# Loading order and early tiles at the opening of a one-core attention and gated-MLP kernel

## The chip, the cores and the metric

One core of a Trainium2 chip runs the whole program in one launch. The metric is the device time of one execution in microseconds. Three runs of the kernel before gave 556.28, 556.47 and 556.8, median 556.47. The engines are called PE (matrix products), PEld (PE's weight loads), DVE, ACT, POOL and SP; SP issues most transfers.

## The reference, cut to what matters

The input x has 2048 rows of 576. It is normalized per row, and two branches take the result: windowed causal attention (32 heads of 18, window 256) with an output product, and an MLP whose gate is a sigmoid. The output is x + attention * silu(MLP).

```python
def _A_ref(x, wqkv, wo):
    H = 32; Dh = D // H; W = 256
    q, k, v = qkv[0], qkv[1], qkv[2]
    scores = jnp.einsum("bhqd,bhkd->bhqk", q, k) * (Dh ** -0.5)
    mask = (idx[:, None] - idx[None, :] >= 0) & (idx[:, None] - idx[None, :] < W)
    p = _softmax(jnp.where(mask[None, None], scores, -1e9), axis=-1)
    return (lambda x, *d: x.transpose(*d))(o, 0, 2, 1, 3).reshape(B, S, D) @ wo

def _B_ref(x, w_gate, w_up, w_down):          # D = 576, F = 4608
    h = _sigmoid(g) * u                       # g = x @ w_gate, u = x @ w_up
    return jnp.einsum("bsf,fd->bsd", h, w_down)

xn = _layernorm(x, axis=-1)
s = _A_ref(xn, A_wqkv, A_wo)
g = _silu(_B_ref(xn, B_w_gate, B_w_up, B_w_down))
return x + s * g
```

## The kernel before

The rows are taken in four stretches (`c`, 512 rows each, four blocks of 128). In each stretch x is normalized and transposed to `xnT`; then come the v and q/k products, 40 tiles of scores with their exponentials on ACT and masks on DVE, two runs of PV products (L817), the output product of attention, 36 tiles of gate and up ("F tiles", 128 hidden units each), and the down products with the final combination.

**Products in pairs.** The contraction of 576 is split into four blocks of 128 and a remainder of 64. Every matmul uses 64 rows of the array, and `pair` (L123) issues two of them that run side by side. A gate/up tile is two turns: `lo` (four pairs, the 128-row blocks) and `hi` (the same four for the other halves, and the pair of the remainder, `wgr`). The second turn waits for the first, so PE does another turn in between where one is at hand.

**The planner.** `build_graph` lists operations with dependencies, estimates and priorities. `schedule` (L1125) then places them one by one on the engines, each on the engine's earliest start plus 10 ns for each step of priority, and so fixes the order of every engine; `emit` writes the program in that order, with waits on semaphores. On the chip an engine never overtakes: an operation that is late holds all behind it on its engine. The planner's estimates have no other effect than on this order.

**PSUM.** There are four units of two banks each. `pool_s` (units 0 and 1) serves transposes, q/k, v, scores and the attention output; `pool_f` (2, 3 and 1) serves F tiles and down products; `pool_v` all four, for PV. A unit is taken by the operation that comes first and given back by the copy that empties it (L361 to L363). The planner bars a pool from a unit that a more urgent claim of the other wants.

**The opening** (stretch 0). SP issues by priority: the four x blocks (`load_x`, `X_PRIO`, L70), then the weights of tiles 0 and 1 (gate, up, and the remainders with `REM_PRIO`), then the next groups of two tiles (`weights`, L923). Each x block is normalized on its own (`build_ln`, L525): statistics on DVE, block 2's on ACT (`STATS_ACT`), a power on POOL, the normalization and a 64-column duplicate on DVE, ten small transposes on PE (L613), and a copy from PSUM to `xnT` on the engine that `XE_ENG` names (L590). The statistics of the fourth block have a low priority (`LN_PRIO`, 16). Until the first transposes PE runs products on zeros (`NWARM` pairs, L490). Then the first `NEARLY` F tiles are made in parts, so that PE can start on the blocks that are there: `PARTS` (L80) gives the ranges of blocks. Each early tile holds its own PSUM unit until its last part, and the `lo` turn of the following tile, `ahead` (L995), is put in front of the last part's `hi`.

**Instruction loads.** PE's program is read in pieces of 256 instructions. A PV run is very dense in instructions, and `fits` (L1113) lets it start only where the next piece has, by the planner's reckoning, the time `FETCH_NS` to arrive. `SPACE_NS` is the least distance between score tiles that the planner aims at, `FILL_NS` how much it pays for it, `POOL_IN_NS` the margin for a unit's release.

Of the kernel before, what the change touches and what calls it, by code (L numbers as in the profile page):

```python
# [8 lines left out]
D = 576  # L9
# [37 lines left out]
RUN_NS = 6.3  # L47
STEP_NS = (54.0, 30.6)
# [21 lines left out]
X_PRIO = (0, 0, 0, 0)  # L70
# [4 lines left out]
XE_ENG = ("ACT", "ACT", "ACT", "DVE")  # L75
NWARM = (43, 10)
NEARLY = 2
FIRST_SLACK_NS = (-800.0, -1500.0)
BUSY_SLACK_NS = 1500.0
PARTS = (((0, 1), (1, 2), (2, 3), (3, 4)),) * NEARLY  # L80
# [10 lines left out]
POOL_IN_NS = 140.0  # L91
DMA_PE_NS = 690.0
FILL_NS = 100.0
SPACE_NS = (1700, 1800, 1700, 1700)
# [101 lines left out]
class Op:  # L196
    __slots__ = ("eng", "est", "deps", "fn", "name", "prio", "start", "end", "tok", "needs_tok",
                 "nbytes", "slack", "idx", "succs", "cidx", "odeps", "acq", "lane", "filler", "space", "ni", "run", "then")

    def __init__(self, eng, est, fn, name, deps, prio, nbytes, odeps, acq):  # L200
        self.eng = eng
        self.est = float(est)
        self.fn = fn
        self.name = name
        self.deps = []
        seen = set()
        stack = list(deps)
        while stack:
            d = stack.pop(0)
            if d is None:  # L210
                continue
            if isinstance(d, (list, tuple)):
                stack = list(d) + stack
            elif id(d) not in seen:
                seen.add(id(d))
                self.deps.append(d)
        self.prio = prio
        self.start = None
        self.end = None
        self.tok = None  # L220
        self.needs_tok = False
        self.nbytes = nbytes
        self.idx = -1
        self.succs = []
        self.cidx = -1
        self.odeps = [d for d in odeps if d is not None]
        self.acq = acq
        self.lane = None
        self.slack = 0.0
        self.filler = None  # L230
        self.space = 0.0
        self.ni = 0
        self.run = 0
        self.then = None
        for d in self.odeps:
            assert d.eng == eng
# [22 lines left out]
class Builder:  # L259
# [40 lines left out]
    def alloc_memory(self):  # L300
# [61 lines left out]
        self.pool_f = Pool("F", [2, 3, 1], last)  # L362
# [55 lines left out]
    def load_x(self, c, i=0):  # L418
        if c == 0:
            for i in range(BPC):  # L420
                self.x_dma[i] = (self.dma(self.x0[:, i, :], self.x[i * P:(i + 1) * P, :], P * D * 2, f"dma:x{i}", ("x0", i), prio=X_PRIO[i]),
                                 self.x0[:, i, :])
                self.x_dma[i][0].slack = -220.0
# [20 lines left out]
    def load_rem(self, dst, srcs, name, lane, prio, deps=()):  # L444
        return [self.dma(dst[ROWS[1 - t], :], src[0:RD, :], RD * src.shape[1] * 3, name, lane + (t,), deps=deps, prio=prio)
# [150 lines left out]
    def act_stats(self, x_in, o_x, pr):  # L596
# [4 lines left out]
        m = op("POOL", 150, lambda e: e.tensor_scalar(nm, sx, -1.0 / D, None, ALU.mult), "ln:am", deps=[a1], prio=pr)  # L601
        a2 = op("ACT", act_ns(D) + 150, lambda e: e.activation(junk, x_in, ACTF.Square, bias=nm, accum_out=sq), "ln:aq", deps=[m], prio=pr)
        v = op("POOL", 150, lambda e: e.tensor_scalar(ve, sq, 1.0 / D, EPS, ALU.mult, ALU.add), "ln:av", deps=[a2], prio=pr)
# [301 lines left out]
    def build_ffn(self, c):  # L905
# [17 lines left out]
        def weights(wg):  # L923
# [14 lines left out]
            if c == 0:  # L938
                for d in ds:
                    d.slack = FIRST_SLACK_NS[0] if wg == 0 else BUSY_SLACK_NS if wg > 6 else 0.0  # L940
                for d in rem:
                    d.slack = FIRST_SLACK_NS[1] if wg < 2 else BUSY_SLACK_NS if wg > 6 else 0.0

# [10 lines left out]
        def gate_up(ft, h, half, acq, part=None, deps=(), behind=()):  # L954
# [8 lines left out]
            def f(eng):  # L963
                return turn(eng, [bank(h, w)[:, t0:t0 + n] for w in range(2)], lhs, lambda r, t, k: x_in[r, k, t0:t0 + n], half)
            o = op("PE", len(BLOCKS[half]) * mm_ns(n), f, f"f1{half}:{c}:{ft}", deps=[xin, wops[ft // WG][0:1 + half], deps],
                   prio=3 if part is None else 1, odeps=chain[half] if part is None else list(behind), acq=acq,
# [19 lines left out]
        if early:  # L986
# [3 lines left out]
            for ft, h in enumerate(hs):  # L990
                u = None
                for part in range(len(PARTS[ft])):
                    lo = gate_up(ft, h, 0, None if part else h, part, [u])
                    if ft == early - 1 and part == len(PARTS[ft]) - 1:
                        ahead = self.pool_f.hold()  # L995
# [117 lines left out]
    def fits(self, at, n, st, places, ffn):  # L1113
# [5 lines left out]
        while edge - FETCH - FETCH_AHEAD < at + n:  # L1119
            if edge > at and when(edge) - when(edge - FETCH - FETCH_AHEAD) < FETCH_NS[ffn]:  # L1120
# [4 lines left out]
    def schedule(self):  # L1125
# [13 lines left out]
        last_sc = 0.0  # L1139
        at = 2  # L1140
# [5 lines left out]
        while nsched < len(ops):  # L1146
            best = None
            for e in ENGS:
# [10 lines left out]
                for o in cand:  # L1159
# [3 lines left out]
                    if o.run and not self.fits(at + len(self.new_waits(o, known)) // 2, o.run, st, places, int(ffn[phase] < FETCH)):  # L1163
# [52 lines left out]
            if o.lane is not None:  # L1216
# [3 lines left out]
                bw_clock = max(bw_clock, stt + o.est) + o.nbytes / DMA_BYTES_PER_NS  # L1220
            else:
# [120 lines left out]
```

## Time and profile before

| what | us |
|---|---|
| profiled execution, device time | 556.48 |
| its span | 555.2 |
| PE busy | 549.9 (99%) |
| DVE busy | 325.1 (59%) |
| ACT busy | 271.7 (49%) |
| POOL busy | 208.8 (38%) |
| first product on real data starts | 7.98 |
| first product of 512 columns starts | 12.23 |
| last product ends | 552.7 |

How to read it: times within the execution count from the span's start. Busy shares are averages over the whole span. The chain that ended last is followed back from the last instruction, at each step to what released it. In a row of the timeline stand the start, the length, engine and line, the operation, what it writes and reads, how many instructions are merged in the row, and in brackets the idle time before it with what ended it. Idle time of an engine that is not the bottleneck costs nothing.

### The profile page before, as it was taken

How to read it: one execution, taken by the hardware profiler on the slowest of the kernel's cores; microseconds unless marked ns; L12 is line 12 of the kernel's file. 1: busy time of each engine (PE TensorE's matmuls, PEld its weight loads, DVE VectorE, ACT ScalarE, POOL GpSimd, SP SyncE). 2: the span in 40 equal slices, each digit the busy share in tenths (PEclk: the TensorE clock that was granted, in tenths of full speed). 3: DMA queues.
4: the chain of work that ended last, by engine and by line, in shares of the span. 5: the costliest groups of instructions: out<-in, count | busy, mean ns of one | idle time of the engine just before them, and what ended most of it. 6: DMA issues, size and time to landing. Idle time of an engine off the chain costs nothing.

```text
span 555.2 us, 19412 instructions
## 1 busy us (share of the span) xinstructions
PE 549.9 (99%) x8342; PEld 341.2 (61%) x8342; DVE 325.1 (59%) x782; ACT 271.7 (49%) x379; POOL 208.8 (38%) x360
## 2 busy tenths in 40 slices
PE   8999999999999999999999999999999999999998
PEld 7454455777555655577855565447877655445887
DVE  5467677745966545746565557664455657653511
ACT  4246554432566543645265563764165555765021
POOL 5634353826271230554452322745063332700300
DMA  8899999542256664462126653663013464540001
GB/s 230 234 263 239 248 241 257 150 91 59 72 164 182 198 167 132 129 161 53 32 65 193 201 162 101 185 179 87 9 34 103 119 204 138 153 134 2 20 28 46
DMA packets 141213, 75.87 MB, mean 137 GB/s; under 512 B 43676, under 2 KB 139260, under 8 KB 141128
## 3 DMA queue, kind: packets, MB, share of 16 engines
q1 hardware_dynamic: 133704, 68.71, 47.3%
q0 software_dynamic: 7424, 5.92, 4.0%
q8 instruction: 66, 1.08, 0.8%
q14 instruction: 19, 0.16, 0.1%
HBM read 63.18 MB, written 2.36 MB: 118 GB/s over the span
## 4 chain that ended last, share of the span: by engine, by line
PE 98%; DMA 1%; SPq 0%; issue 0%; DVE 0%; ACT 0%
PE ps L127 95%; PE ps L817 3%; DMA wgs<-in_B_w_up_dram 1%; SPq L290 0%; ACT thf L1087 0%; PE ps L613 0%; DVE thf L1089 0%; DVE xf L1092 0%
## 5 line engine op out<-in xcount | busy, mean ns | idle before, releaser
L127 PE MATMUL ps<-xnT,wgs 64*128 64x512 bf16 (+1 forms) x2400 | 284.0, 368 | 0.6 <-DMA wgs<-in_B_w_up_dram 0.5
L767 ACT ACTIVATE expr<-ps 128x1024 bf16<-128x1024 f32 (+4 forms) x160 | 155.0, 968 | 81.0 <-PE ps L127 80.5
L127 PEld LDWEIGHTS ps<-xnT,wgs 64*128 64x128 bf16 x2400 | 114.7, 94 | 108.6 <-issue 1.1
L127 PE MATMUL ps<-wd_sb,hT 64*128 64x288 bf16 (+2 forms) x2448 | 152.7, 276 | 0.0
L290 POOL DMA_DIRECT2D qk<-qd x160 | 82.9, 524 | 161.7 <-PE ps L127 152.9
L977 DVE SCALAR_TENSOR_TENSOR hT<-tring,ps 128x512 bf16<-128x512 bf16 x144 | 98.6, 685 | 74.2 <-ACT tring L974 72.6
L974 ACT ACTIVATE tring<-ps 128x512 bf16<-128x512 f32 x144 | 86.2, 598 | 113.9 <-PE ps L127 112.3
L127 PEld LDWEIGHTS ps<-wd_sb,hT 64*128 64x128 bf16 x2448 | 113.0, 94 | 29.4
L780 DVE TENSOR_TENSOR expr<-expr,mask 128x128 bf16<-128x128 bf16 (+2 forms) x240 | 65.2, 299 | 62.0 <-ACT expr L767 59.4
L290 POOL DMA_DIRECT2D oT<-o2T x72 | 36.8, 520 | 115.3 <-DVE ot L848 52.4
L731 POOL TENSOR_SCALAR kx<-kprev,small 128x256 bf16<-128x256 bf16 x64 | 60.1, 949 | 6.0 <-PE ps L127 5.1
L127 PE MATMUL ps<-qk,kx 64*128 64x320 bf16 (+1 forms) x704 | 59.2, 254 | 0.0
L127 PE MATMUL ps<-xnT,wgr 64*128 64x512 bf16 (+1 forms) x300 | 56.0, 367 | 0.0
L127 PEld LDWEIGHTS ps<-qk,kx 64*128 64x128 bf16 x704 | 31.9, 94 | 26.6
L127 PE MATMUL ps<-xnT,wqg 64*128 64x512 bf16 (+1 forms) x320 | 37.7, 355 | 0.0
L652 DVE CAST qd<-ps 128x1024 bf16<-128x1024 f32 (+1 forms) x20 | 22.3, 1115 | 11.1 <-PE ps L127 11.1
L845 DVE STREAM_TRANSPOSE ot<-ps 128x512 f32<-128x512 f32 x32 | 20.3, 687 | 13.9 <-PE ps L817 13.8
L127 PEld LDWEIGHTS ps<-xnT,wgr 64*128 64x128 bf16 x300 | 15.0, 94 | 16.4
L731 DVE TENSOR_SCALAR kx<-qk,small 128x512 bf16<-128x512 bf16 x64 | 21.9, 370 | 5.4 <-PE ps L127 4.9
L853 DVE STREAM_TRANSPOSE o2T<-o 128x512 bf16<-128x512 bf16 x32 | 22.6, 706 | 3.0 <-DMA oT<-o2T 2.5
L127 PEld LDWEIGHTS ps<-xnT,wqg 64*128 64x128 bf16 x320 | 15.0, 94 | 11.5 <-issue 0.4
L1080 ACT ACTIVATE thf<-ps 128x576 bf16<-128x576 f32 x12 | 7.8, 650 | 27.4 <-PE ps L127 27.4
(68 smaller groups left out, 289.3 us busy)
## 6 DMA issues: line engine op xcount, KB each, us to landing
wgs<-in_B_w_gate_dram SPq DMA_DIRECT2D x72, 256.0 KB, 3.5
wgs<-in_B_w_up_dram SPq DMA_DIRECT2D x72, 256.0 KB, 4.0
wd_sb<-in_B_w_down_dram SPq DMA_DIRECT2D x9, 576.0 KB, 6.7
wqg<-in_A_wqkv_dram SPq DMA_DIRECT2D x32, 128.0 KB, 3.8
qk<-qd POOLq DMA_DIRECT2D x100, 36.0 KB, 2.7
wgr<-in_B_w_gate_dram SPq DMA_DIRECT2D x36, 64.0 KB, 3.1
wgr<-in_B_w_up_dram SPq DMA_DIRECT2D x36, 64.0 KB, 2.9
wvo<-in_A_wqkv_dram SPq DMA_DIRECT2D x4, 576.0 KB, 4.2
```

What stands on the lines that cost most here:

```text
L127: res = eng.matmul(outs[i], lhs(ROWS[t], i), rhs(ROWS[t], i), start=start, stop=stop, tile_position=(64 * t, 0))
L290: o = self.op(eng, DMA_ISSUE_NS[eng], lambda e: e.dma_start(dst, src), name, deps, prio, nbytes=nbytes)
L652: return eng.tensor_copy(dst, self.both(h, n))
L731: return e.tensor_scalar(self.kx[:, sx, pos:pos + n_ // SW, t, :], src.rearrange("p (s k) -> p s k", k=SW), self.half[:, t:t + 1], None, A ...
L767: return eng.activation(self.expr[:, se, :, lo * SW:NT], self.both(h, NT)[:, :, lo * SW:NT], ACTF.Exp, scale=SM_SCALE)
L780: return eng.tensor_tensor(e_, e_, m_, ALU.mult)
L817: res = eng.matmul(outs[i][p0:p0 + VH, cols], self.v_aug[ROWS[i], o:o + VH], self.expr[ROWS[i], se, t, cols], start=m == 0, stop=m == len( ...
L845: return e.transpose(self.ot1[:, p1, :], self.halves(hp, NT, un)[i])
L853: t2 = op("DVE", dve_ns(NT), lambda e, p2=p2, p3=p3: e.transpose(self.o2T[:, p3, :], self.o2[:, p2, :]), f"ot2:{c}:{pr}:{i}", deps=[on, d3 ...
L974: th = op("ACT", act_ns(NT), lambda e: e.activation(self.tring[:, st, :], bank(h, 0), ACTF.Tanh, scale=0.5), f"th:{c}:{ft}", deps=[pg, dt_ ...
L977: mu = op("DVE", dve_ns(NT), lambda e: e.scalar_tensor_tensor(self.hT[:, ft, :], self.tring[:, st, :], 1.0, bank(h, 1), ALU.add, ALU.mult) ...
L1080: th = op("ACT", act_ns(w), lambda e: e.activation(v2(t), y2(), ACTF.Tanh, scale=0.25), f"fth:{nm}", deps=[f2, dt_], prio=0)
```

## The change

Five things are edited.

1. The fourth x block's load gets the priority 1.8, which puts it behind the first gate, up and remainder weights and in front of the second weight group.
2. `NEARLY` goes from 2 to 3; the third early tile has two parts, blocks 0 to 2 together and block 3. Parts of early tiles get a priority that grows with the tile.
3. The first block's copy from PSUM moves from ACT to DVE (`XE_ENG`).
4. `pool_f` takes unit 0 as well, as its last choice; the tile run ahead in the opening is confined to unit 0 (`pool_a`).
5. The planner's numbers: the landing of the opening's transfers is now estimated by a running sum of bytes and a latency for each (`OPEN_NS`, `X_LAT_NS`, `W_LAT_NS`), score tiles are spaced by 1900 to 2000 ns, a unit's margin is 120 ns, two estimates on POOL are larger, there is one more warm-up pair, and the rule for PV runs relaxes with the time that a run has waited (`RELAX_NS`).

```diff
RUN_NS = 6.3
+RELAX_NS = 200e3
 STEP_NS = (54.0, 30.6)
...
 LN_PRIO = (0, 0, 0, 16)
-X_PRIO = (0, 0, 0, 0)
+X_PRIO = (0, 0, 0, 1.8)
 REM_PRIO = 0.6
...
 DUP_ACT = ()
-XE_ENG = ("ACT", "ACT", "ACT", "DVE")
-NWARM = (43, 10)
-NEARLY = 2
-FIRST_SLACK_NS = (-800.0, -1500.0)
+XE_ENG = ("DVE", "ACT", "ACT", "DVE")
+NWARM = (44, 10)
+NEARLY = 3
+OPEN_NS = 2000.0
+OPEN_BYTES_PER_NS = 256.0
+X_LAT_NS = (400.0, 600.0, 900.0, 800.0)
+W_LAT_NS = (650.0, 1100.0)
 BUSY_SLACK_NS = 1500.0
-PARTS = (((0, 1), (1, 2), (2, 3), (3, 4)),) * NEARLY
+PARTS = (((0, 1), (1, 2), (2, 3), (3, 4)),) * 2 + (((0, 3), (3, 4)),)
 NQK = 5
...
 PE_IN_NS = 60.0
-POOL_IN_NS = 140.0
+POOL_IN_NS = 120.0
 DMA_PE_NS = 690.0
-FILL_NS = 100.0
-SPACE_NS = (1700, 1800, 1700, 1700)
+FILL_NS = 130.0
+SPACE_NS = (1900, 1900, 2000, 1900)
 DMA_BYTES_PER_NS = 280.0
...
     __slots__ = ("eng", "est", "deps", "fn", "name", "prio", "start", "end", "tok", "needs_tok",
-                 "nbytes", "slack", "idx", "succs", "cidx", "odeps", "acq", "lane", "filler", "space", "ni", "run", "then")
+                 "nbytes", "slack", "idx", "succs", "cidx", "odeps", "acq", "lane", "filler", "space", "ni", "run", "then", "lat")
 
...
         self.then = None
+        self.lat = None
         for d in self.odeps:
...
         self.pool_s = Pool("S", [0, 1], last)
-        self.pool_f = Pool("F", [2, 3, 1], last)
+        self.pool_f = Pool("F", [2, 3, 1, 0], last)
+        self.pool_a = Pool("F", [0], last)
         self.pool_v = Pool("V", [0, 1, 2, 3], last)
...
                                  self.x0[:, i, :])
-                self.x_dma[i][0].slack = -220.0
+                self.x_dma[i][0].lat = X_LAT_NS[i]
             return
...
     def load_rem(self, dst, srcs, name, lane, prio, deps=()):
-        return [self.dma(dst[ROWS[1 - t], :], src[0:RD, :], RD * src.shape[1] * 3, name, lane + (t,), deps=deps, prio=prio)
+        return [self.dma(dst[ROWS[1 - t], :], src[0:RD, :], RD * src.shape[1] * 2, name, lane + (t,), deps=deps, prio=prio)
                 for t, src in enumerate(srcs)]
...
         a1 = op("ACT", act_ns(D) + 150, lambda e: e.activation(junk, x_in, ACTF.Identity, accum_out=sx), "ln:as", deps=[o_x, self.op_tab], prio=pr)
-        m = op("POOL", 150, lambda e: e.tensor_scalar(nm, sx, -1.0 / D, None, ALU.mult), "ln:am", deps=[a1], prio=pr)
+        m = op("POOL", 230, lambda e: e.tensor_scalar(nm, sx, -1.0 / D, None, ALU.mult), "ln:am", deps=[a1], prio=pr)
         a2 = op("ACT", act_ns(D) + 150, lambda e: e.activation(junk, x_in, ACTF.Square, bias=nm, accum_out=sq), "ln:aq", deps=[m], prio=pr)
-        v = op("POOL", 150, lambda e: e.tensor_scalar(ve, sq, 1.0 / D, EPS, ALU.mult, ALU.add), "ln:av", deps=[a2], prio=pr)
+        v = op("POOL", 290, lambda e: e.tensor_scalar(ve, sq, 1.0 / D, EPS, ALU.mult, ALU.add), "ln:av", deps=[a2], prio=pr)
         rs = op("POOL", 560, lambda e: e.tensor_tensor(self.arstd[:, :], ve, self.neghalf[:, :], ALU.pow), "ln:ar", deps=[v, self.op_negh], prio=pr)
...
             if c == 0:
-                for d in ds:
-                    d.slack = FIRST_SLACK_NS[0] if wg == 0 else BUSY_SLACK_NS if wg > 6 else 0.0
-                for d in rem:
-                    d.slack = FIRST_SLACK_NS[1] if wg < 2 else BUSY_SLACK_NS if wg > 6 else 0.0
+                for d in ds + rem:
+                    d.slack = BUSY_SLACK_NS if wg > 6 else 0.0
+                    if wg < 4 and d.lat is None:
+                        d.lat = W_LAT_NS[min(wg, 1)]
 
...
             o = op("PE", len(BLOCKS[half]) * mm_ns(n), f, f"f1{half}:{c}:{ft}", deps=[xin, wops[ft // WG][0:1 + half], deps],
-                   prio=3 if part is None else 1, odeps=chain[half] if part is None else list(behind), acq=acq,
+                   prio=3 if part is None else 1 + ft / 2, odeps=chain[half] if part is None else list(behind), acq=acq,
                    ni=4 * len(BLOCKS[half]))
...
                     if ft == early - 1 and part == len(PARTS[ft]) - 1:
-                        ahead = self.pool_f.hold()
+                        ahead = self.pool_a.hold()
                         ahead = (ahead, gate_up(early, ahead, 0, ahead))
...
 
-    def fits(self, at, n, st, places, ffn):
+    def fits(self, at, n, st, places, ffn, waited):
         def when(p):
...
         while edge - FETCH - FETCH_AHEAD < at + n:
-            if edge > at and when(edge) - when(edge - FETCH - FETCH_AHEAD) < FETCH_NS[ffn]:
+            if edge > at and when(edge) - when(edge - FETCH - FETCH_AHEAD) < FETCH_NS[ffn] * (1.0 - waited / RELAX_NS):
                 return False
...
         last_sc = 0.0
+        moved = OPEN_NS
         at = 2
...
                     st = max(free[e], ready_t[o.cidx])
-                    if o.run and not self.fits(at + len(self.new_waits(o, known)) // 2, o.run, st, places, int(ffn[phase] < FETCH)):
+                    if o.run and not self.fits(at + len(self.new_waits(o, known)) // 2, o.run, st, places, int(ffn[phase] < FETCH), st - ready_t[o.cidx]):
                         continue
...
                 bw_clock = max(bw_clock, stt + o.est) + o.nbytes / DMA_BYTES_PER_NS
+                if o.lat is not None:
+                    moved = max(moved, stt + o.est + 700.0) + o.nbytes / OPEN_BYTES_PER_NS
+                    o.end = moved + o.lat
             else:
```

## The prediction

> **What bounds the kernel now.** I read the page's 40 slices first, then the chain that ended last, in order of time, then the list of PE's own waits, and last the timeline of the first 16 us.
>
> The first two lines are from the page (PE's busy tenths; shares of the chain), the others are pieces of the chain (start, length, what):
>
> ```profile
> PE   8999999999999999999999999999999999999998
> PE 98%; DMA 1%; SPq 0%; issue 0%; DVE 0%; ACT 0%
> ...
> 3.14 4.71 DMA wgs<-in_B_w_up_dram
> 7.84 0.14 issue
> 7.98 1.00 PE ps L127 x26
> 8.98 0.14 PE ps L613 x10
> 9.13 1.30 PE ps L127 x45
> 10.43 0.14 PE ps L613 x10
> 10.58 73.81 PE ps L127 x810
> ...
> 336.28 1.48 PE ps L817 x100
> 337.75 0.09 issue
> ```
>
> To be seen: until 7.84 us the first up-weights are on their way; from 7.98 to 552.7 the chain is PE alone. A faster engine, or a transfer that lands earlier, after 8 us gives nothing. Only the start of PE's work, holes in PE and the tail after 552.7 count.
>
> PE's waits are few (total us, times, longest):
>
> ```profile
> PE ps L613 <- DVE xnr L561: 1.1, 2, 0.8
> PE ps L127 <- DMA wgs<-in_B_w_up_dram: 0.5, 1, 0.5
> ```
>
> Holes too short for that list I took from the distances between matmul starts (a pair of 512 columns starts every 216 ns, of 128 columns every 56). After 7.98 they sum to 0.18 us in the opening (the largest, 0.105, before the first use of the remainder weights at 8.4), 0.23 at 87.9, 0.23 inside the PV run at 336.3 (it takes 2.63 us, the other five of its size 2.40), 0.10 at 427.0, 0.06 at 325.7, and about 0.09 at the entry of each of the eight PV runs, which stay. So what can be won after the opening is about 0.62 us.
>
> The opening, from the timeline:
>
> ```profile
> 0.80 1.82 SPq L290 DMA_DIRECT2D x<-in_A_x_dram  x4
> 2.66 0.43 SPq L290 DMA_DIRECT2D wgs<-in_B_w_gate_dram  x1
> ...
> 5.69 0.72 PE L127 MATMUL ps<-hT 64*128 64x128 bf16 x20
> 5.70 0.45 DVE L541 BATCH_NORM_STATS2 small<-x 128x6 f32<-128x288 bf16 x1
> ...
> 6.49 0.68 ACT L590 ACTIVATE xnT<-ps 128x640 bf16<-128x640 bf16 x1
> ...
> 7.18 0.32 PE L613 MATMUL ps<-ident,xnr 64*128 64x64 bf16 x10 [0.76 <-DVE xnr L561]
> ...
> 8.18 0.20 DVE L545 BATCH_NORM_AGGREGATE small<-small 128x2 f32<-128x12 f32 x1
> ...
> 10.62 0.49 DVE L590 COPY xnT<-ps 128x640 bf16<-128x640 bf16 x1 [0.22 <-PE ps L613]
> ```
>
> To be seen: four x blocks are issued before the first weights; the fourth block's statistics run at 5.70 and then lie until 8.18; the first block's copy is done at 7.17, 0.67 us before the weights.
>
> **The change, part by part.** The sum is made against the profiled execution, 556.48 us (span 555.2 and 1.28 around it), which is also within 0.01 us of the median of the runs.
>
> *x block 3 behind the first weights.* Its DMA issue (0.43 us on SP) and its 144 KB (147,456 B) leave the queue ahead of the first gate, up and two remainder transfers. From 4 to 6 us the DMA moved 269 GB/s, so all four land 0.55 us earlier: up at 7.29 instead of 7.84, the last remainder at 7.80 instead of 8.35. Total bytes up to the second weight group are the same, so that lands as before (gate 9.27, up 10.47). Add the 0.14 us of the chain's "issue" line: first real matmul at 7.43. Gain 0.55. One step of sixteen in each semaphore is late in this trace (up: fifteen by 6.97, the last at 7.84); I keep that lateness in both kernels.
>
> *First block's copy on VectorE.* On DVE it costs 0.49 by the row at 10.62, on ACT 0.68. DVE is free for it: it replaces the fourth block's statistics (5.70 to 6.51), so it runs at about 5.9 to 6.4. The copy ends 0.8 us earlier, but that alone is not on the path: 7.17 was already before 7.43. Worth 0 to 0.05; I take 0.
>
> *The fourth block's own chain, now late.* It lands where the last remainder did, about 8.4. From its landing: statistics 0.84, aggregate and variance 0.47, POOL power 0.58, normalize 0.47, duplicate 0.24, so its transposes can start at 11.0 (2.6 after landing); transposes 0.32 and the DVE copy 0.49 give its xnT at 11.9; before it was 11.1. What covers it: after 7.43 PE has two early tiles on blocks 0 to 2, each 9 pairs x 56 ns, 3.02 us in all; the transposes of blocks 1 and 2 at 0.14 each; and the third tile's part on blocks 0 to 2, 9 pairs of 384 columns, 1.46 us, whose weights are there at 10.6. Together that reaches 12.2, past 11.9. But PE runs in a fixed order. By the planner's rules (priority 0 for a transpose, 2 for the third tile) the fourth transposes are likely to be put ahead of the third tile; PE would come there at 10.73 and wait until 11.0, then about 0.1 for the copy. So the wait is 0 (order the other way) to 0.4; I take 0.25. If x lands later, it grows one for one.
>
> *Block 1's transposes* (0.14 in PE's chain) lay before 7.98, in the wait for the weights; priority puts them behind the first four pairs now, so they move into the counted time: 0 to +0.14, I take 0.12. *Third early tile:* 384 + 128 columns instead of 512 adds 9 x 2.5 ns = 0.02. *One more warm-up filler* lies before 5.5, in front of the first transposes: 0. *The hole before the remainder weights* at 8.4 and the smaller ones: they land 0.55 earlier while PE reaches them 0.4 earlier; -0.18 to 0, I take -0.15.
>
> *F tiles on all PSUM units.* A gate/up tile keeps its unit for 1.94 of PE, 0.2 of latency and the tail of ACT and DVE (0.60 + 0.69): about 3.4 us, of a period of 1.94, that is 1.75 units. Three are enough; the fourth is for the tile run ahead in the opening. Later it takes no hole away that the trace shows. The reverse, attention's tiles finding both their units taken, would cost only if PE had nothing else; gate/up and down products fill it to 510 and 552. I take 0.
>
> *Planner constants* (wider spacing of score tiles, 20 ns less margin for a unit's release, a fetch rule that relaxes with waiting, other DMA estimates). Score tiles start 2.16 us apart at the median, above the old 1.7 to 1.8 and the new 1.9 to 2.0, so in gate/up the rhythm stays; beside the down products one more piece of 0.49 comes between. The attention output product of the last stretch ends at 540.6, 12 us before PE's end; 40 score tiles x 0.2 = 8 us still fits. The margin: 160 score tiles and 20 q/k tiles x 20 ns bound its loss at 3.6 us, but no such wait shows among PE's; nearest row 0, and the new order cannot take back more than the 0.62 of holes. So -0.62 to +1.9 (the PV rival below); I take 0, since each old hole may vanish and as many new ones appear.
>
> Sum: -0.55 + 0.25 + 0.12 + 0.02 - 0.15 = -0.31, so 556.48 - 0.31 = 556.17; rounded 556.2. The tail after PE (ACT 0.31, DVE 0.25 and 0.24, the last store) is not touched.
>
> **The rivals.**
>
> *Fourth block too late, gain eaten.* Against the sum above: if x lands after 8.9, the wait is 0.75 or more and the opening gives back all: 556.5 to 557.2. For it: the late steps of the semaphores; against it: 1.46 us of third-tile work that may stand ahead.
>
> *Slower: a PV run waits for its instructions.* The run at 336.3 stood still for 0.23 us with every operand ready ("issue" at 337.75 in the chain). Two 16 KB loads of PE instructions around a PV run start 3.4 to 3.9 us apart in the trace, while a run of 2.40 us uses up more than one such load, 256 of its 384 instructions in 1.6 us. A badly placed run can thus stand 3.5 - 1.6 = 1.9 us. The change moves all of them and lets one that has waited long start with less margin. One full case gives 556.48 - 0.31 + 1.9 = 558.1; it is slower by 1.1 from 1.4 us of such waiting in the eight runs. Against it: seven of eight show none.
>
> *Slower: PE's clock falls back.* The warm-up pairs of 128 columns start every 107 ns until 4.3 us and every 56 afterwards, so 3.3 us at half rate. With block 1's transposes moved behind the first products, PE stands from 6.3 to 7.4, 1.1 us in one piece; before, 0.93 and 0.65 did no harm. If it fell back, 3.3 us at half rate lose 1.65: 557.8. The Trainium skill, "TensorE: Matmul & The Clock Gate", Part 1, says that the clock goes to half only after a window of about 3.4 us without work; by that rule 1.1 us is harmless, and the trace's 0.93 agrees.
>
> *Faster than that.* No wait at the transposes, no inserted ones, and all four later holes gone: -0.55 - 0.18 - 0.62 = -1.35: 555.1.
>
> **How the numbers follow.** About 0.2% (1.1 us) is what a measurement of this kernel can tell from no change. My forecast, a small gain of the opening and nothing after: 0.52 (own range 555.5 to 556.7). Fourth block too late: 0.16. Both lie within 0.2%: 0.68. PV runs 0.13 and clock 0.03: slower 0.16. Everything at once: faster 0.16. Range: down to 555.1 for the good case, up to 557.9, which takes in the clock and the milder half of the PV case; about 0.07 lie above and 0.07 below.
>
> **What would show it.** First real product at about 7.4, not 7.98; the fourth x block's statistics at about 8.4; transposes of it near 11.0 with a short wait before them; the first 512-column product near 12 as before or earlier; PE's end 0.3 earlier than 552.7. A PE start that is not earlier, a wait over 0.6 before the fourth transposes, or "issue" pieces of over 0.3 at PV runs would make it wrong.

## The result, and the profile after

The changed kernel takes 563.89 us (median of four runs, 562.87 to 564.23), the kernel before, beside it on the same chip, 556.38 (556.18 to 556.8). The ratio is 1.0131, 95% interval 1.0113 to 1.0149: slower by 1.3%, or 7.5 us, where 556.2 with a range up to 557.9 was forecast. The profiled execution took 562.87, its span is 561.6, 6.4 longer than the one before. It is the fastest of the four; the account that follows is of this one.

From the page of the changed kernel, PE's busy tenths in 40 slices and the chain's shares:

```profile
PE   8999997999999999999999999999999999999998
PE 98%; issue 1%; DVE 0%; ACT 0%
```

One digit has changed: the seventh slice, 84 to 98 us, has a 7 where there was a 9. "issue", 0% before, has 1% of the chain. The chain of the changed kernel (start, length, what) says where:

```profile
7.67 0.22 PE ps L131 x8
7.89 1.00 issue
8.89 0.73 PE ps L131 x20
...
62.19 0.61 ACT tring L980
...
62.82 0.70 DVE hT L983
...
86.83 4.18 PE ps L131 x46
91.01 1.78 PE ps L823 x123
92.79 3.25 issue
96.04 0.21 PE ps L823
96.25 46.96 PE ps L131 x664
```

To be seen: the first PV run (L823; a run of this size takes 1.79 us) begins at 91.01 (in the kernel before at 84.39, where the chain has it in one piece, `84.39 1.79 PE ps L817 x124`), and before its last products PE stands still for 3.25 us with nothing that it waits for in the profile. There is a hole of 1.00 us at 7.89 in the opening. PE's own waits in this kernel (total, times, longest) give the same three places:

```profile
PE ps L823 <- issue: 3.2, 1, 3.2
...
PE ps L131 <- issue: 1.0, 1, 1.0
PE ps L131 <- DVE hT L983: 0.5, 1, 0.5
```

The windows around the first PV run of the changed kernel (stretch and length, busy time of PE, PEld, DVE, ACT and POOL, granted clock, DMA share, GB/s):

```profile
86.00:92.60 6.60, 6.60 (x182) 4.29 (x179) 3.94 (x10) 2.29 (x4) 4.32 (x7) 1.00 1.13 294
92.60:96.00 3.40, 0.19 (x24) 0.04 (x6) 0.99 (x2) 0.00 (x0) 0.00 (x0) 0.97 1.10 292
96.00:99.30 3.30, 3.26 (x17) 1.17 (x18) 2.62 (x5) 0.00 (x0) 0.00 (x0) 0.51 1.16 263
99.30:104.00 4.70, 4.70 (x52) 2.14 (x48) 2.35 (x7) 2.92 (x4) 0.00 (x0) 1.00 0.45 128
```

To be seen: while PE stands, the DMA engines are full (share 1.10, 292 GB/s). Behind the stall the granted clock is 0.51 for a stretch: the clock's record puts it at half from 95.82 on for 3.41 us. Seven pairs of 512 columns lie there, 427 ns apart instead of 216.

To lay out the 6.4 us I took, for both executions, the start of a product less the column time of all real products before it (a pair of n columns n/2.4 + 2.4 ns): the time in which PE made nothing useful. It is 8.28 before and 8.88 after at 20 us, 8.34 and 9.78 at 82, 8.94 and 15.17 at 100, 12.04 and 18.32 at 550; only the differences are used. So the opening gave +0.6, the stretch from 20 to 82 us +0.84 (0.5 of it the third wait above), the first PV run and what follows +4.8 (some 3.3 of standing and 1.5 of half clock), and the 450 us after that nothing. The other three executions have a mean granted clock of 0.993 to 0.994 where this one has 0.997. One stretch of 3.41 us at half is worth 0.003 of the mean, so by this estimate they had two such stretches; that fits a median that is 1.0 above the profiled time.

The opening, from the timeline of the changed kernel:

```profile
7.05 0.40 PE L131 MATMUL ps<-xnT,wgs 64*128 64x128 bf16 x8
7.51 0.39 PE L131 MATMUL ps<-xnT,wgs 64*128 64x128 bf16 x8
8.89 0.40 PE L131 MATMUL ps<-xnT,wgs 64*128 64x128 bf16 x8 [1.00 <-issue]
9.11 0.23 PE L131 MATMUL ps<-xnT,wgr 64*128 64x128 bf16 x2
9.18 0.46 DVE L547 BATCH_NORM_STATS2 small<-x 128x6 f32<-128x288 bf16 x1 [0.95 <-DMA x<-in_A_x_dram]
11.80 0.32 PE L619 MATMUL ps<-ident,xnr 64*128 64x64 bf16 x10
```

To be seen: the first real product starts at 7.05, 0.93 earlier than before. Then PE stops from 7.89 to 8.89 for the remainder weights (`wgr`): fifteen of the sixteen steps of their semaphore had come by 7.49, the last at 8.80. The fourth block's statistics begin at 9.18, its transposes at 11.80, with no wait of PE in front of them.

### The profile page after: what moved, and what is told of

It is laid out like the page before. It is cut to its first block, busy times and chain, and to the rows that moved or that the text cites. A ratio compares the mean times of both kernels' runs of the same rounds, so it can differ in the third digit from the quotient of the medians.

```text
span 561.6 us, 19453 instructions
## 1 busy us (share of the span) xinstructions
PE 553.1 (98%) x8362; PEld 349.4 (62%) x8362; DVE 323.7 (58%) x783; ACT 270.7 (48%) x378; POOL 208.6 (37%) x360
## 4 chain that ended last, share of the span: by engine, by line
PE 98%; issue 1%; DVE 0%; ACT 0%
PE ps L131 95%; PE ps L823 3%; PE ps L619 0%; DVE hT L983 0%; ACT tring L980 0%; ACT thf L1093 0%; DVE thf L1095 0%; DVE xf L1098 0%; DVE hT L464 0%; DVE small L465 0%
## 5 line engine op out<-in xcount | busy, mean ns | idle before, releaser
L131 PE MATMUL ps<-xnT,wgs 64*128 64x512 bf16 (+1 forms) x2416 | 287.1, 368 | 1.7 <-issue 1.0
L131 PEld LDWEIGHTS ps<-xnT,wgs 64*128 64x128 bf16 x2416 | 118.4, 94 | 112.1 <-issue 8.0
L131 PEld LDWEIGHTS ps<-wd_sb,hT 64*128 64x128 bf16 x2448 | 115.1, 94 | 27.0
L131 PEld LDWEIGHTS ps<-qk,kx 64*128 64x128 bf16 x704 | 33.1, 94 | 24.9
L823 PE MATMUL ps<-expr,v_aug 64*19 64x320 bf16 (+4 forms) x1408 | 18.7, 254 | 3.2 <-issue 3.2
```

The lines of the kernel that those rows point to most:

```text
L131: res = eng.matmul(outs[i], lhs(ROWS[t], i), rhs(ROWS[t], i), start=start, stop=stop, tile_position=(64 * t, 0))
L823: res = eng.matmul(outs[i][p0:p0 + VH, cols], self.v_aug[ROWS[i], o:o + VH], self.expr[ROWS[i], se, t, cols], start=m == 0, stop=m == len( ...
```

## The experiments

**The theory.** PE outruns the loading of its own program in the first PV run, which the new order puts at a bad place while the DMA engines are full; the clock falls because PE stands. **The rivals:** that the order itself (late x block, third early tile, spacing, PSUM units) costs the time somewhere else; that the loss belongs to single executions; that a certain number of the planner is at fault.

For the loads I read the trace's instruction queue. The page has 66 loads of 16 KB on it, and PE's program has two instructions (weight load and product) per matmul record and semaphore instructions between them (264 in the kernel before), 16949 in all: a load is a piece of 256. Counted so, every stall of 0.2 us or more in or behind a PV run that has nothing to wait for lies where PE comes to a multiple of 256 plus 193. A load's first packet never came earlier than about 1.0 to 1.1 us after PE had passed the place 320 instructions ahead of such an end, in any execution; I take that passing as the time of asking, which no record shows. "Stood" is the chain's "issue" piece at that place; all is in us, and the experiments that the rows belong to follow:

```
kernel          end of piece  asked   packet  PE there  asked-packet  packet-PE  asked-PE  stood
before           2497          84.83   88.42   92.82     3.60          4.40       8.00      -
before           9921         331.37  335.46  337.85     4.10          2.38       6.48      0.09
after            2497          88.04   93.60   96.18     5.57          2.58       8.14      3.25
after again      2497          87.69   93.13   95.85     5.44          2.72       8.16      3.29
old spacing      2497          89.14   95.27   97.90     6.13          2.63       8.76      3.50
64 places on     2497          84.00   90.72   93.42     6.71          2.71       9.42      1.38
light weights    2497          86.83   89.66   91.98     2.83          2.32       5.15      0.28
larger margin    2497          87.13   92.12   95.85     4.99          3.73       8.72      -
spacing alone    2497          87.85   91.56   93.89     3.70          2.33       6.04      0.74
x late alone    11201         376.02  379.57  382.08     3.54          2.51       6.05      1.02
```

Wherever PE stood, it went on 2.3 to 2.7 us after the load's first packet; in the two rows where it did not stand it came to the end of the piece 3.7 and 4.4 after it. So the stall is the wait for the load. What differs is the way from asking to packet: in the first 95 us it is 3.4 to 4.8 us in the mean of each execution and 5.1 to 7.9 at most, from 100 us on 2.1 to 2.4 in the mean. Over all thirteen traces its median is 1.7 where the DMA engines were less than a tenth busy around the asking, and 3.7 where they were over nine tenths.

**1. The program moved by 64 instructions.** Sixteen more warm-up pairs in the second group of them, of which the planner knows nothing, so that the plan stays and every piece ends 64 instructions earlier in it:

```diff
-        def f_warm(eng):
-            return pair(eng, ...)
+        def f_warm(eng, more=0):
+            for _ in range(more + 1):
+                res = pair(eng, ...)
+            return res
...
+            f = (lambda e: f_warm(e, MORE)) if before and i == 3 and n == NWARM[1] else f_warm
```

> The changed kernel with 16 more warm-up pairs in its second warm-up group, which its planner does not know of: the order of all that follows is the same, but every later PE instruction lies 64 places further on in the 256-instruction pieces. Theory A (an instruction load that comes late at a piece's end): the first PV run now meets the end of its piece 192 instructions in instead of 256, the load is asked for about 8 us earlier than needed instead of 4.5, and took about 8; so the stall of 3.4 us near 92.6 goes to 0 to 0.5, and with it the half clock behind it (1.5 us or more). The later runs lose margin (second end at about 425 instead of 485, asked for 3 to 4 us ahead): stalls of 0 to 1.2 us appear inside or just behind several of the six runs of 384 instructions, 0.5 to 4 us in all. The extra pairs cost 0 to 1.5 us in the opening. Time 559 to 564. Theory B (the stall belongs to the work at that place: a buffer or an operand): the stall stays at the end of the first PV run with 3 us or more, no new ones inside the later runs, time 564 to 565.5.

561.81 (560.52 to 563.45), ratio 1.0092 (1.007 to 1.0115). The first run in the chain of this kernel:

```profile
90.59 1.45 PE ps L827 x95
92.04 1.38 issue
93.42 0.62 PE ps L827 x31
```

The stall has moved with the end of the piece (123 products of the run lie ahead of it in the changed kernel's chain, 95 here), and it is 1.38 instead of 3.25: the load was asked for 8.0 us before PE came to the end of the piece, there 4.8. More than the 0 to 0.5 that I expected was left, since this load's packet took 6.71. The clock stayed full. In exchange, smaller stops of 0.13 to 0.31 came in or behind later runs, PE waited 0.6 for up weights just before 86.4, and the total fell by 2 us only. A stall that hung on an operand or a buffer of the plan would not have moved.

**2. Fewer bytes beside it.** The gate and up weights of tiles 20 to 35 of the first stretch and 0 to 7 of the second are loaded to a quarter; the order is that of the changed kernel.

```diff
+        if few:
+            return self.dma(dst[:, 0, :], src[RD:RD + P, :], ...)
...
+            few = c == 0 and wg > 9 or c == 1 and wg < 4
```

> The changed kernel, same order and same instruction places, but the gate and up weights of tiles 20 to 35 of the first stretch and of tiles 0 to 7 of the second are loaded to a quarter (one of four row blocks), so less is moved between about 50 and 110 us; the products of those tiles use what the buffers held before. Theory A with the load slow because the DMA is full: the load of the piece starts 1.2 to 3 us after it is asked for instead of 5.6, the stall near 92.6 is 0 to 1 us instead of 3.4 and the clock stays at full: 557.5 to 560. If the place alone makes the stall, whatever else is moved: 3 us or more, 563 to 564. Theory B: unchanged, 563 to 564.

558.22 (557.19 to 559.15), ratio 1.0026 (1.0016 to 1.0036). The chain of this kernel:

```profile
89.81 1.78 PE ps L825 x123
91.59 0.28 issue
91.87 0.19 PE ps L825
```

Same run, same place among the instructions, and 0.28 instead of 3.25: the packet came 2.83 us after the asking instead of 5.57. So the traffic beside it is what makes this load late, and the half clock is gone with the stall. The share of busy DMA engines alone does not tell how late a load will be: from asking to packet it was 1.14 in the changed kernel (304 GB/s, 5.57 us), 1.17 in the kernel before (227 GB/s, 3.60 us), and 0.45 (130 GB/s) for a load that took 5.2 us in experiment 7. The excess over the kernel before is 1.4 us instead of 7.5.

**3. A larger margin for the first stretch.** The changed kernel with a third entry in the rule for PV runs, 8500 ns in place of 4350 in the first stretch, and with it a third entry for the time that an instruction behind the run takes:

```diff
-FETCH_NS = (6200.0, 4350.0)
+FETCH_NS = (6200.0, 4350.0, 8500.0)
...
-STEP_NS = (54.0, 30.6)
+STEP_NS = (54.0, 30.6, 54.0)
...
-... places, int(ffn[phase] < FETCH), st - ready_t[o.cidx]):
+... places, 2 if phase == "0" else int(ffn[phase] < FETCH), st - ready_t[o.cidx]):
```

> The changed kernel with one planner rule stricter: in the first stretch a PV run may start only where 8.5 us lie between the asking for a piece and its need (instead of 4.35). The plan puts the first run with a piece's end 167 instructions in, 8.9 us ahead. Theory A: no stall over 0.5 us in the first run and no half clock; what is left against the kernel before is the opening (+0.6 in the profile) and small holes: 556.5 to 559. Theory C (the loss is in the opening and the new order as a whole, and the stall only the form that it took): 562 to 564.

558.03 (557.29 to 559.54), ratio 1.0019 (1.001 to 1.0029). The chain of this kernel:

```profile
7.88 0.99 issue
...
44.02 50.84 PE ps L131 x510
94.85 1.79 PE ps L823 x124
96.64 49.46 PE ps L131 x740
```

The run starts later, the load has 8.7 us, and neither stall nor half clock is there. Time without useful products is 8.85 by 20 us and 13.0 by 550. So a kernel with all five edits and without the stall is 1.2 us slower than before, about half of it visible in the opening (+0.57). Two independent edits, 2 and 3, bear the theory out for about 6 of the 7.5 us.

**4. Only the wider spacing.** The kernel before with `SPACE_NS` (1900, 1900, 2000, 1900).

```diff
-SPACE_NS = (1700, 1800, 1700, 1700)
+SPACE_NS = (1900, 1900, 2000, 1900)
```

> The kernel before with one edit, the distances of score tiles (1900, 1900, 2000, 1900 instead of 1700, 1800, 1700, 1700). Opening unchanged. The plan moves the first PV run from 83.6 to 89.4, a piece's end then lies 24 instructions behind its end, asked for 4.7 us ahead. Theory A: a stall of 2.5 to 3.5 us just behind the first PV run, and the clock halves behind it if the stall fills a window: 558.5 to 563. Theory C: the opening is that of the kernel before, so 556 to 557.

558.75 (558.23 to 559.94), ratio 1.0037 (1.0023 to 1.0052). The chain of this kernel:

```profile
91.96 1.19 PE ps L127 x11
93.15 0.74 issue
...
216.16 1.49 PE ps L817 x101
217.65 0.74 issue
218.39 1.05 PE ps L817 x76
```

The opening is as before (8.26 by 20 us). The spacing moves PV runs, and two loads come late: one behind the first run, one in the run at 216. The first of these stalls is where I expected it, but 0.74 instead of 2.5 to 3.5: this load's packet took 3.70, not 5.57.

**5. The changed kernel again.** No edit.

> The changed kernel itself once more. If the late load is a fixed property of its order, the first PV run stands still again at its last matmul, by 3 us or more, the clock record shows at least one window at half behind it, and the time is 562 to 564.5. If the first profile was an accident: no stall over 1 us there, 557 to 560.

563.16 (561.05 to 564.32), ratio 1.0116 (1.0093 to 1.0138). It stands for 3.29 us from 92.44 on. The window behind that:

```profile
95.70:99.10 3.40, 3.37 (x33) 1.56 (x34) 2.62 (x5) 0.23 (x1) 0.00 (x0) 1.00 0.74 172
```

The stall belongs to the kernel, not to an execution. The half clock does not come every time: this profiled execution, 561.05, kept the full clock, and the three others, 563.0 to 564.3, have a mean granted clock of 0.997. Nor does the hole at 62.8 belong to it (9.40 by 20 us, 9.62 by 82). In the opening PE waited 1.5 us at the fourth block's transposes instead: they started at 12.33, the block's last step having come at 9.69.

**6. The changed kernel with the old spacing.**

```diff
-SPACE_NS = (1900, 1900, 2000, 1900)
+SPACE_NS = (1700, 1800, 1700, 1700)
```

> The changed kernel with the old distances of score tiles (1700, 1800, 1700, 1700). The plan puts the first PV run at 88.7 with a piece's end 5 instructions behind its end, asked for 4.6 us ahead. If the place of the run against the pieces is what counts, the stall stays, just behind the run, 2.5 to 4 us, with a half clock if it passes 3.4: 560 to 564. If the wider spacing by itself is the cause, the stall goes: 557 to 558.5.

563.32 (561.54 to 566.32), ratio 1.0128 (1.0095 to 1.0161). The two windows of this kernel behind its first run, with the granted clock in the third column from the end:

```profile
94.40:97.90 3.50, 0.01 (x2) 0.00 (x1) 1.46 (x3) 0.00 (x0) 0.00 (x0) 0.79 1.17 287
97.90:103.30 5.40, 5.40 (x26) 1.97 (x28) 1.56 (x4) 1.19 (x2) 0.00 (x0) 0.50 0.80 186
```

The stall is still there, 3.50 us just behind the run, and the profiled execution had twice the stretch of half clock (6.83 us from 96.44 on). In this execution PE also waited 1.6 us for remainder weights before 62.4 and 0.4 for `hT` before 65.0, so not all of its 566.32 belongs to the stall. The spacing is not the cause; it only picks the place, as 4 picked another one.

**7. Everything but the late x block,** with the margin of 3.

```diff
-X_PRIO = (0, 0, 0, 1.8)
+X_PRIO = (0, 0, 0, 0)
```

> The third experiment's kernel (stricter margin in the first stretch) with the fourth x block in front of the weights again; three early tiles and the rest stay. Theory: the late fourth block and the late remainders cost the opening about 0.3 to 0.6 us against the kernel before (time without useful products by 20 us: 8.85 in the third experiment, 8.28 in the kernel before). Then this one stands at 8.2 to 8.5 by 20 us, the transposes of block 3 start without a wait, and the time is 0.2 to 0.6 below that of the third experiment. Rival: the third early tile and the priorities cost it: 8.7 to 9.0 as before, no gain.

557.65 (556.48 to 559.07), ratio 1.002 (1.0011 to 1.003). Time without useful products by 20 us is 8.15, 0.7 less than in 3 and 0.13 less than before: the third early tile, the copy on DVE and the one more filler cost nothing. The 0.7 is one pair of executions, and most of it is the wait for the remainder weights (0.99 in 3, 0.40 here). Over the eight traced openings with the late block the figure is 8.25 to 9.40, in the mean 8.8; in the five without it, 8.15 to 8.28, in the mean 8.2. So the late block costs the opening about 0.6 us, from nothing to 1.2. The gain did not come out of the total, because another load was late. The chain of this kernel:

```profile
348.30 1.47 PE ps L823 x98
349.77 1.07 issue
350.84 1.06 PE ps L823 x78
```

**8. The fourth block's transposes behind the third tile,** with the margin of 3 and the late block.

```diff
-            tr = op("PE", KB * 29.5, ..., prio=0, acq=h, ni=20)
+            tr = op("PE", KB * 29.5, ..., prio=0 if i < 3 else 12, acq=h, ni=20)
```

> The third experiment's kernel with a lower priority for the transposes of block 3 alone, so that PE does the first half of the third early tile ahead of them. Theory (PE waits in order for a late block): the wait of 0.5 to 0.7 us before these transposes, where the remainders were in time, goes to 0 to 0.1, and the lost time by 20 us falls by 0.3 to 0.6 against the third experiment where that wait was there. Rival: block 3 is needed right behind anyway, so the wait only moves to its first products: 0 to 0.1 gained.

557.87 (557.21 to 560.58), ratio 1.0033 (1.002 to 1.0046). Inconclusive: no wait is left in front of those transposes, but neither was there one in the profile of 3, where the wait for the remainder weights (0.99) had come first; here that wait was 1.34 (their last step at 9.16), and the time by 20 us 9.08.

**9. Only the late x block,** in the kernel before, and **10. the same once more.**

```diff
-X_PRIO = (0, 0, 0, 0)
+X_PRIO = (0, 0, 0, 1.8)
```

> The kernel before with one edit, the fourth x block loaded behind the first gate, up and remainder weights. Two early tiles, everything else as before; the plan's first PV run has 6.2 and 8.0 us of margin. Theory (a late fourth block costs the opening more than the earlier start gives): PE starts on real data near 7.0 to 7.5 instead of 7.98, but waits for block 3 with nothing to do; time without useful products by 20 us 8.8 to 10 against 8.2 to 8.3, time +0.5 to +1.8. Rival (the earlier weights win): 7.7 to 8.1 by 20 us, time -0.1 to -0.6.

Of four executions the traced one took 1500 us, so its trace says nothing of the cause; the other three took 561.67 to 562.0, the kernel before 556.84: five us slower, far over what I expected. For the cause, once more:

> The kernel before with only the fourth x block put behind the first weights, once more, since the first time no usable trace was left; its times were 561.7 to 562.0, five above the kernel before, at a full granted clock. My theory (PV runs outrun the loading of PE's instructions): its plan starts the first PV run near 82.4 us, at another place among PE's instructions, so most of the 5 us is a stall of PE of 2 to 4 us with operands ready inside or just behind the first PV run, the load under way for 8 us, and perhaps one of 0.3 to 1 us at a later run; the opening loses 0.4 to 1.3 against the kernel before. Rival (the opening): the time without useful products by 20 us is 12 or more instead of 8.3, and no stall over 1 us follows. Rival (tail): PE's last product ends within 1.5 us of the kernel before and the span is longer behind it. Time 561.5 to 562.5.

561.23, beside 556.19 (one execution of each); span 559.9, granted clock 1.0 throughout. The chain of this kernel:

```profile
379.42 1.63 PE ps L817 x109
381.06 1.02 issue
...
502.20 1.66 PE ps L817 x113
503.86 0.61 issue
```

And its timeline at the end:

```profile
531.56 0.65 ACT L899 ACTIVATE s_attn<-ps 128x576 bf16<-128x576 f32 x1 [2.41 <-PE ps L127]
532.23 1.28 ACT L1087 ACT_TABLE_LOAD   x1
533.52 0.65 ACT L1087 ACTIVATE thf<-ps 128x576 bf16<-128x576 f32 x1
534.23 1.16 PE L127 MATMUL ps<-wvo,oT 64*128 64x288 bf16 x16 [0.75 <-ACT thf L1087]
```

My theory had the mechanism and missed the place. The first run is undisturbed (1.79 us at 83.16); the opening lost 0.67 (the first product of 512 columns starts at 12.90 instead of 12.23; 0.58 of it is a wait for the fourth block's `xnT`, though that block had landed at 7.53), the late runs at 379 and 502 stood 1.02 and 0.61, and 0.9 us (0.75 by the row) went where PE waits for ACT to empty a unit: ACT's load of a function table, 1.28 us, lies at 511.0 in the kernel before, with 13.8 us of ACT's idle time behind it, and here at 532.23, right in front of that copy. These four are 3.2 of the 4.7 us of span. The rest is spread over pieces under 0.4 that I have not put down to anything. The opening was not the main part, so that rival fell too.

**11. Only the fourth unit for F tiles,** in the kernel before.

```diff
-        self.pool_f = Pool("F", [2, 3, 1], last)
+        self.pool_f = Pool("F", [2, 3, 1, 0], last)
```

> The kernel before with one edit, F tiles may take unit 0 as their last choice. The first six PV runs keep their places against the pieces; the order changes only in the last stretches. Expected: nothing in the opening, no new stall in PV runs over 0.3 us, time within 0.8 of the kernel before. If the fourth unit by itself starves the score tiles: +1 or more, with holes of PE in the score rhythm.

558.72 (558.01 to 559.02), ratio 1.0032 (1.0019 to 1.0044): 1.9 us slower, more than the 0.8 that I allowed, and neither a PV run nor a hole among the score tiles is the reason. PE's last product ends at 552.49, 0.2 earlier than before, and yet the span is 1.6 longer. The timeline of this kernel's tail:

```profile
548.08 2.77 SPq L290 DMA_DIRECT2D xf<-in_A_x_dram  x2
552.09 0.45 DVE L1092 TENSOR_TENSOR xf<-xf,thf 128x576 bf16<-128x576 bf16 x1
553.03 0.52 DVE L1092 TENSOR_TENSOR xf<-xf,thf 128x416 bf16<-128x416 bf16 x2
554.17 1.31 SPq L290 DMA_DIRECT2D out_dram<-xf  x3
```

The last blocks of x for the residual are fetched at 548.08 here and at 540.69 before. The addition to the first of them stands at 552.09 in DVE's order, among the last blocks' work (548.14 before), and all three last stores leave in a row from 554.17, where the first of them left at 548.69 before. In the changed kernel the tail is as long as before (2.5 us behind PE's end), so this cost is not part of its 7.5 us.

**12. The parts that looked harmless together:** the changed kernel with x first, the old spacing and the margin of 3.

```diff
-X_PRIO = (0, 0, 0, 1.8)
+X_PRIO = (0, 0, 0, 0)
...
-SPACE_NS = (1900, 1900, 2000, 1900)
+SPACE_NS = (1700, 1800, 1700, 1700)
```

> The changed kernel without its three costs: the fourth x block in front of the weights again, the old distances of score tiles, and the stricter margin for PV runs in the first stretch. By the runs so far the opening is then worth 8.15 by 20 us against 8.2 to 8.3, the PV runs have 4.3 us or more where loads took 3.5 to 4.2, and 8.85 in the first stretch. Expected 556.0 to 557.2, the same as the kernel before; if the third early tile and the fourth unit are worth something, 555.6 to 556.2.

557.94 (557.3 to 561.17), ratio 1.0032 (1.0015 to 1.0048). Above the 556.0 to 557.2 that I expected. The opening is as short as in 7 (8.15 by 20 us), but the first run, now at 82, stood 0.44 (its load was asked for 9.0 us before PE came there, and the packet took 6.9), and before 107.6 PE waited 0.3 for a transfer of `qk`. The rest of the 2.0 us of span is spread over holes under 0.4. No version beat the kernel before.

## Why the prediction was wrong, point by point

- **First real product at 7.43.** It came at 7.05, so this step was right in sign. Fifteen of the up weights' sixteen steps came 0.58 earlier, as reckoned (6.38 instead of 6.96); the rest of the 0.93 is luck, since the last step lagged by 0.07 here and by 0.88 in the trace of before. Nor was the 7.98 that I started from a fixed size: experiments 4 and 11 have the opening of the kernel before, and there the up weights landed at 7.46 and 6.90 and the first real product started at 7.59 and 7.57, with no gain by 20 us (8.26 and 8.22). An earlier start is worth nothing by itself, neither there nor here, where PE stands at the next weights.
- **The hole before the remainder weights, -0.15.** Wrong in sign in this execution. I let them land at 7.80, the 8.35 of before less 0.55, with the late step (1.02 there) in it; fifteen steps had come by 7.49, the last at 8.80, and PE waited 1.00. What failed is the assumption that the lateness is the same in both kernels and moves with the queue: the up weights lost theirs, the remainder's grew to 1.31. In the second profile the remainder landed at 7.76, and there was no such wait.
- **Fourth block: statistics at 8.4, transposes at 11.0, wait 0.25 (0 to 0.4).** Mis-sized. Statistics at 9.18, transposes at 11.80; in the second profile 9.71 and 12.33, with a wait of 1.5. The way from landing to transposes was right (2.64 from 9.16, 2.64 from 9.69, forecast 2.6); the landing was late by its last step (fifteen had come by 7.80 and 7.48). The rival "fourth block too late" (x after 8.9 us, a wait of 0.75 or more) is what the opening of the second profile did. In the first one its number came true by another way: x landed at 9.16, but PE had lost the time at the remainder weights and did not wait for the block.
- **Copy on DVE, third tile, filler, block 1's transposes: together +0.14.** Right as far as can be seen for the first three: -0.13 by 20 us in experiment 7, where block 1's transposes (7.27) still lie before the first real product (7.43). The order that I put together for PE (block 1's transposes behind the first four pairs, the fourth block's before the third tile) is the order of the program.
- **F tiles on all units: 0.** Right for the changed kernel, whose later stretches lose nothing. By itself the edit made the tail 1.7 us longer, which I had not thought of: I looked for PSUM waits only, and the edit acts through the order.
- **Planner constants: 0, between -0.62 and +1.9.** This is the step that failed: the term for the PV runs, put at 0 in the sum. The upper end was one badly placed PV run, priced at 3.5 - 1.6 = 1.9 us; the run measured 3.25 of standing and 1.5 of half clock. The 3.5 was the distance of two loads around late runs (around the first run of the same trace it is 7.3 and 6.4 us), and such a distance tells how fast PE uses its program up, not how long a load takes. What PE has to wait for is the way from asking to going on: 8.1 us at the first run of the changed kernel, against 6.0 to 6.5 in the two rows above that lie behind 300 us. The trace of before had it: for the first run's piece the load was asked for at 84.83 and its packet came at 88.42, and the end of the piece was reached 8.0 us after the asking, with no time lost. That run was undisturbed because it was well placed, not because the matter is harmless. `fits` asks for 4.35 us there, and the run of the changed kernel had 4.75, so by the measured times the rule passes it without `RELAX_NS`; that number, the unit's margin and the new transfer estimates were not tried alone.
- **The chance of that rival, 0.13, from "seven of eight runs show none".** Too low. The places of one plan are no sample of the next plan's: of the nine other orders, or placings of one order, that were profiled, six have an "issue" piece of 0.4 us or more in or just behind a PV run.
- **Clock falls back: 0.03, as a case by itself, in the opening.** PE stood 1.0 us there and the clock stayed full. By the rule of the Trainium skill, "TensorE: Matmul & The Clock Gate", Part 1, only a window of about 3.4 us without work halves it; the trace agrees there. But the case does not stand by itself: the fall came during a stall of 3.25 us, and experiment 2, without the stall, has none. It belonged to the PV rival as a second price, 1.5 us.

With the stall priced from the first 95 us, 3.3, the half clock, 1.5, and the late block's opening, +0.6, the sum against the profiled 556.48 would have been 561.9; the profiled execution took 562.87, and 0.8 of the rest is the stretch from 20 to 82 us, half of it a hole that the second profile does not have.

## What to carry to other kernels

Where a program's order is made by a planner, an edit acts on every later place too: look at what each dense run of instructions has to spare for the next piece of program, and price a miss from loads in the same stretch of the execution, with the DMA engines as full as they are there. A run without a stall in one order says nothing about another order. A gain at the start of PE's work counts only up to the next transfer that it needs, and of that it is the last of the sixteen steps that counts.

## What the runs showed of the hardware that I had not expected

- The program of PE comes by DMA, and the traffic of the data slows it down. At a share of 1.14 (304 GB/s) a 16 KB piece took 5.6 us from asking to its packet, with the weights beside it cut to a quarter 2.8; from the packet to PE's going on it is 2.3 to 2.7 us in every row above in which PE stood.
- The granted clock went to half for stretches of 3.41 us (once 6.83). The length of the stall did not decide alone: PE had stood 3.0 us when it fell in the first profile (92.79 to 95.82), 2.0 in experiment 6 (94.41 to 96.44), and after 3.29 us in experiment 5 it did not fall. The Trainium skill, "TensorE: Matmul & The Clock Gate", Part 1, gives the window as 3413 ns and says that it runs freely; the 3.41 agrees, and in both traces with such a fall it came a whole number of such stretches after the clock's first rise (26 from 7.07 to 95.82, 27 from 4.28 to 96.44). The last stretch before the fall had PE at work for 0.39 us in the first profile and for 1.38 in experiment 6, so a window need not be wholly empty. Where the windows of experiment 5 lay, no record shows.
- The last of a transfer's sixteen steps can come long after the other fifteen, and how long differs between executions of one kernel: 1.31 us for the remainder weights and 1.36 for the fourth block in the first profile, 0.94 and 2.21 in the second, and 0.07 for the up weights in the first. Why is open.
